# A linear-attention and ReLU network of four layers on one core: one more chunk of the first dense layer in seven block products, with the weight sums, the room of x and the GpSimd choices that go with it

## The chip, the cores and the metric

One NeuronCore of a Trainium2 chip runs the whole kernel. The metric is the device time of one execution in microseconds, as a median over runs. The core has a matrix engine (TensorE, PE in the profile, with PEld for its weight loads), a vector engine (VectorE, DVE), an activation engine (ScalarE, ACT), a general engine (GpSimd, POOL) and SyncE (SP), which here issues every DMA. The engines run their own instruction lists in order and wait for each other by semaphores.

## What is computed

The input x is 2048 x 512 in bf16. Four layers are applied: attention, dense, attention, dense, each on a layer norm of x and added to x. Both attention layers share their weights, and so do both dense layers. Cut to what matters:

```python
qkv = x @ wqkv                        # 32 heads of 16
phi = lambda t: where(t > 0, t + 1, exp(t)) + 1e-6
pq, pk = phi(q), phi(k)
kv  = einsum("bhsd,bhse->bhde", pk, v)
den = einsum("bhqd,bhd->bhq", pq, sum_s(pk))
A   = (einsum("bhqd,bhde->bhqe", pq, kv) / den) @ wo
B   = relu(x @ w1) @ w2               # 512 -> 1376 -> 512
x = x + A(layernorm(x)); x = x + B(layernorm(x))   # twice
```

## The kernel before

The 2048 rows are 16 tiles of 128, four tiles to a chunk, so four chunks 0 to 3. Layers are numbered 0 to 3; 0 and 2 are attention, 1 and 3 dense. x stays in SBUF as `xres` (f32); the bf16 input of layer 0 is `xin`, its normalised form `xn`, and the transposed form that TensorE needs `Tb`. All large intermediate values lie in `big`, cut into units of 512 columns: in attention layers the k features (16 units), the q features (16) and the spread reciprocal denominators (16); in dense layers the hidden values h, unit 4c + t for feature block c of 11 and chunk t.

An attention layer projects k for each tile and q for each chunk, forms G = xn' phi(k) (`a_g`), from it K'V under a mask and the product with `wo` (`a_kv`, `a_m`), the denominators (`a_den`), spreads their reciprocals over partitions by four DMAs for each chunk (`a_spread`, L779), scales q by them (`a_pqs`, L786), multiplies (`a_fin_mm`) and adds to x with the row sums for the next norm (`resid`, L657). The step `bar` of `layer_steps` is where the four chunks meet.

A dense layer forms h for each chunk (`h_step`) and then its output (`o_step`, `b_out`). The output, 256 x 256 blocks of rows and columns in a 2 x 2 scheme, is done in Winograd's form of Strassen's method: seven block products in place of eight, with sums of blocks made ahead of it by VectorE (`w2_sums` for the weights, `b_out_sums` for h) and after it from PSUM. For h there are two forms. `b_h` (L949) is the plain one: ten groups of four matmuls of 512 columns and a relu each. `b_h7` (L875) is the one in seven products: sums of the weights (`w1_sums`, L853), four sums of the transposed input (hs1 to hs4, L888), products of 256 columns, three of which are saved from PSUM by ACT (L926), VectorE adds (L913) and relus (L916, L917, L943, L945). Layer 3 uses it for all chunks and layer 1 from chunk `H7_FROM = 2` on. The last 96 of the 1376 features are apart (`b_h_rest`), turned by a DMA.

The sums of both weights lie in `xin`, in the room of x, which is free once layer 0's residual adds have read it; so they are made when layer 1 runs. One of the four sums of each weight overwrites a block of the weight itself: `usum3` puts b22 - b12 on b12 of w1.

What sets the order: the program writes out all operations with the buffers that they read and write, step by step in an order that `layer_steps` and the loop behind it set; `_list_schedule` (L218) then makes the instruction list of each engine. It is a list scheduler with a duration for every operation (the `C_` constants) and a delay to its consumer (`TAIL`). Among the next `WINDOW` operations of an engine by priority it takes the first that can start, else that with the earliest start. The priority is the operation's number plus an entry of the table `HINTS`; a key with `!` fixes which engine takes an operation that several can do (`add_flex`), by its place in the list of alternatives. Operations in `LOCKED` are laid out so that one on DVE and one on POOL do not overlap. SP's list, the DMAs, is made in the same way with a window of six. The first loads are written at L479 to L506, numbers 0 to 13: x tile 0, x tile 1, wk, x tiles 2 and 3, wq, x chunks 1, 2 and 3, wv, wvl, wo, w1, w2 in two parts.

Every matmul group is emitted at L653, every large GpSimd normalisation at L594; the table load of ACT is at L511.

Of the kernel before, what the change touches and what calls it, by code (L numbers as in the profile page):

```python
# [28 lines left out]
C_ACT_SB_AP = 710.0  # L29
# [17 lines left out]
TAIL = {PE: 150.0, ACT: 125.0, DVE: 80.0, POOL: 40.0, SP: 0.0}  # L47
# [4 lines left out]
WINDOW = {PE: 64, ACT: 80, DVE: 80, POOL: 12, SP: 6}  # L52


HINTS = {"0.bnag10": 2, "0.bnag14": 17, "0.bnst10": -271, "0.bnst12": 80, "0.bnst14": 51, "0.bnst15": 33, "0.bnst6": -82,
# [294 lines left out]
def build_kernel(nc, A_x, A_wqkv, A_wo, B_w1, B_w2, out, n_layers_pairs=2, K_STT=0, Q_STT=0, windows=None,  # L350
# [14 lines left out]
    EPS = 1e-5  # L365
    INV_D = 1.0 / D
    NLAYERS = 2 * n_layers_pairs
    UNITS = max(8 + 4, NFC) * NCH

    es = contextlib.ExitStack()  # L370
    with es:
# [1032 lines left out]
```

## Time and profile before

| | us |
|---|---|
| median of three runs | 268.98 |
| lowest, highest | 268.46, 270.23 |
| the profiled execution | 269.65 |
| its span in the profile | 267.9 |
| DMA: x tile 0 to w2's rest and x chunk 2 landed | 2.94 to 14.53 |

The span is what the profile shows from first to last instruction; some 1.7 us of the execution's time lie around it. The page gives for each engine the time in which at least one of its instructions ran. Rows with a mean in ns give the time of one instruction from start to end; instructions of an engine overlap their neighbours, so a start-to-start distance is shorter than such a row. A wait is put at the engine that stood still, with what released it behind the arrow.

### The profile page before, as it was taken

The numbers are of one execution on the slowest core, as the hardware profiler recorded it, in microseconds if no ns is written. First come the engines' busy times: TensorE is split into PE (matmuls) and PEld (weight loads), VectorE is DVE, ScalarE is ACT, GpSimd is POOL, SyncE is SP. The second block draws the span as 40 slices with busy tenths as digits, with TensorE's granted clock in tenths as the row PEclk, the third lists the DMA queues.
The fourth block names the chain that finished last, engine by engine and source line by source line (L and its number), as shares of the span: only waits on it lengthen the run. The fifth ranks groups of instructions, "written<-read, shape, count | busy, mean of one in ns | idle before, by whom it ended". The sixth has DMA issues, their size and how long they took to land.

```text
span 267.9 us, 5482 instructions
## 1 busy us (share of the span) xinstructions
PE 262.3 (98%) x2020; PEld 183.8 (69%) x2020; DVE 220.5 (82%) x612; ACT 192.0 (72%) x420; POOL 62.8 (23%) x158
## 2 busy tenths in 40 slices
PE   7999999999999999999999999999999999999995
PEld 3665446744646798768687745764488788898884
DVE  5799695679998799698889676348998989899994
ACT  4999987475994467689947599687899886475600
POOL 3210000015678014204005440000760830000000
PEclk9999999999999999999999999999999999999999
DMA  6904490644992400502202222063273221511012
GB/s 201 356 9 92 71 305 0 157 110 88 246 129 51 91 20 4 98 4 39 39 2 39 42 40 39 0 142 96 57 144 79 40 42 42 134 22 78 2 78 81
DMA packets 44890, 22.18 MB, mean 83 GB/s; under 512 B 34784, under 2 KB 43328, under 8 KB 44864
## 3 DMA queue, kind: packets, MB, share of 16 engines
q1 hardware_dynamic: 44864, 21.83, 34.5%
q8 instruction: 16, 0.26, 0.4%
q14 instruction: 10, 0.08, 0.1%
HBM read 7.14 MB, written 2.10 MB: 34 GB/s over the span
## 4 chain that ended last, share of the span: by engine, by line
PE 79%; ACT 8%; DMA 6%; DVE 5%; issue 0%; SPq 0%; DVEq 0%
PE ps L653 79%; DMA Tb<-xn 3%; ACT big L636 2%; ACT sqscr L668 2%; DMA wvl<-in_A_wqkv_dram 2%; DVE xres L660 2%; DMA xin<-in_A_x_dram 1%; ACT escr L638 1%; DVE big L789 1%; ACT Tb L624 1%; ACT xn L599 1%; DVE xn L590 1%; DVE bst L552 1%; ACT xres L638 1%; DVE xn L594 0%
## 5 line engine op out<-in xcount | busy, mean ns | idle before, releaser
L636 ACT ACTIVATE big<-ps 128x512 bf16<-128x512 f32 x64 | 39.7, 644 | 6.1 <-PE ps L653 5.8
L653 PE MATMUL ps<-Tb,w 128*128 128x256 f16 (+1 forms) x216 | 35.8, 304 | 0.1
L668 ACT ACTIVATE sqscr<-xres 128x512 bf16<-128x512 f32 x48 | 30.0, 626 | 6.9 <-DVE xres L1085 4.2
L653 PE MATMUL ps<-w,big 128*128 128x256 bf16 (+1 forms) x256 | 32.4, 272 | 0.0
L653 PE MATMUL ps<-wqkv,Tb 128*128 128x512 bf16 x128 | 31.2, 379 | 0.6 <-DMA Tb<-xn 0.6
L653 PE MATMUL ps<-big,xn 128*128 128x256 bf16 (+1 forms) x224 | 31.6, 288 | 0.0
L653 PE MATMUL ps<-Tb,wqkv 128*128 128x512 f16 (+1 forms) x144 | 31.4, 355 | 0.0
L638 ACT ACTIVATE escr<-ps 128x512 bf16<-128x512 f32 x48 | 29.9, 637 | 1.1 <-PE ps L653 1.1
L653 PE MATMUL ps<-Mf,big 128*128 128x512 bf16 x128 | 29.5, 379 | 0.0
L926 ACT ACTIVATE escr<-ps 128x512 f32<-128x512 f32 (+1 forms) x40 | 20.3, 540 | 11.2 <-PE ps L653 10.9
L653 PEld LDWEIGHTS ps<-w,big 128*128 128x128 bf16 (+1 forms) x256 | 25.0, 98 | 3.7
L653 PEld LDWEIGHTS ps<-big,xn 128*128 128x128 f16 x224 | 21.4, 98 | 8.8 <-issue 0.7
L653 PEld LDWEIGHTS ps<-Tb,w 128*128 128x128 bf16 x216 | 20.8, 98 | 9.5 <-DMA Tb<-xn 1.0
L913 DVE TENSOR_TENSOR big<-ps,escr 128x512 bf16<-128x512 f32 (+1 forms) x40 | 24.0, 606 | 3.7 <-PE ps L653 1.8
L599 ACT ACTIVATE xn<-xres,nbias,rstd 128x512 f16<-128x512 f32 x19 | 15.2, 810 | 9.6 <-POOL nbias L584 6.7
L653 PEld LDWEIGHTS ps<-Tb,wqkv 128*128 128x128 bf16 x144 | 13.9, 98 | 11.9 <-issue 0.2
L653 PEld LDWEIGHTS ps<-Mf,big 128*128 128x128 bf16 x128 | 12.2, 98 | 14.0 <-issue 0.7
L916 ACT ACTIVATE big<-big 128x512 bf16<-128x512 bf16 (+1 forms) x34 | 19.0, 569 | 3.2 <-DVE big L913 2.9
L646 DVE TENSOR_TENSOR big<-big,escr 128x512 bf16<-128x512 bf16 x48 | 19.8, 420 | 1.6 <-ACT big L636 1.1
L653 PEld LDWEIGHTS ps<-wqkv,Tb 128*128 128x128 f16 x128 | 12.1, 98 | 12.8 <-ACT escr L638 1.1
L1066 DVE TENSOR_TENSOR xres<-ps,xres 128x512 f32<-128x512 f32 x24 | 16.4, 685 | 4.6 <-PE ps L653 4.5
L640 DVE TENSOR_SCALAR escr<-escr 128x512 bf16<-128x512 bf16 x48 | 13.7, 287 | 7.7 <-ACT escr L638 7.2
(116 smaller groups left out, 525.2 us busy)
## 6 DMA issues: line engine op xcount, KB each, us to landing
big<-rdc SPq DMA_DIRECT2D x32, 128.0 KB, 2.6
wqkv<-in_A_wqkv_dram SPq DMA_DIRECT2D x3, 512.0 KB, 6.8
xin<-in_A_x_dram SPq DMA_DIRECT2D x3, 512.0 KB, 7.6
w<-in_B_w_dram SPq DMA_DIRECT2D x1, 1376.0 KB, 6.3
w<-in_B_w_dram SPq DMA_DIRECT2D x1, 1280.0 KB, 7.1
wo<-in_A_wo_dram SPq DMA_DIRECT2D x1, 512.0 KB, 7.2
out_dram<-GT SPq DMA_DIRECT2D x1, 512.0 KB, 2.6
out_dram<-Mf SPq DMA_DIRECT2D x1, 512.0 KB, 2.6
```

The lines of the kernel that those rows point to most:

```text
L599: (ACT, lambda e: e.activation(xn[:, i, :], src, ACTF.Identity, scale=rstd[:, i:i + 1], bias=nbias[:, i:i + 1]), C_ACT_SB_AP)],
L636: g.add(ACT, lambda e: e.activation(dst_ap, psv[:, b, :], ACTF.Identity, bias=1.0 + 1e-6, scale=1.0), [("ps", b)], [dst_key], C_ACT_PSUM, ...
L638: g.add(ACT, lambda e: e.activation(sap, psv[:, b, :], ACTF.Exp), [("ps", b)], skeys, C_ACT_EXP, name=name + "_exp")
L640: g.add(DVE, lambda e: e.tensor_scalar(sap, sap, 1.0, 1e-6, ALU.min, ALU.add), skeys, skeys, C_DVE_BF4X, name=name + "_em")
L646: g.add(DVE, lambda e: e.tensor_tensor(dst_ap, dst_ap, sap, ALU.max), [dst_key] + skeys, [dst_key], 340.0, name=name + "_phi")
L653: last = e.matmul(o, l, r, start=st, stop=sp, skip_group_check=skip)
L660: g.add(DVE, lambda e: e.scalar_tensor_tensor(xres[:, i, :], psv[:, b, :], 0.0, src, ALU.add, ALU.add, accum_out=s1[:, i:i + 1]), [("ps", ...
L668: g.add(ACT, lambda e: e.activation(sqscr[:, q, :], xres[:, i, :], ACTF.Square, scale=math.sqrt(INV_D), accum_out=s2[:, i:i + 1]), xr(i), ...
L913: g.add(DVE, lambda e: e.tensor_tensor(ap, sh(psv[:, bank, 0:w]), sh(other()), ALU.add), [("ps", bank)] + okeys + ([] if first else bk), q ...
L916: g.add_flex([(ACT, lambda e: e.activation(ap, ap, ACTF.Relu), C_ACT_PSUM if len(cs) == 2 else 270.0), (DVE, lambda e: e.tensor_scalar(ap, ...
L926: g.add(ACT, lambda e, w=w: e.activation(q[:, 0:w], psv[:, bank, 0:w], ACTF.Identity), [("ps", bank)], key, C_ACT_PSUM if len(cs) == 2 els ...
L1066: g.add(DVE, lambda e: e.tensor_tensor(dst, psv[:, bank, :].rearrange("p (a k) -> p a k", k=256), dst, ALU.add), [("ps", bank)] + keys, ke ...
```

## The change

It does the following, in the diff's order.

- `TAIL` of PE goes from 150 to 160, GpSimd's scheduling window from 12 to 40, and `HINTS` is replaced as a whole. A function gives the price that the scheduler puts on a two-input operation on GpSimd.
- Every ACT operation except the table load reads a key that the table load writes, so all come after it.
- `xin` is no tensor of its own; it is the last 16 of `big`'s 48 units. `tws` and `tw2s` hold the weight sums.
- h units of feature blocks 8 to 10 lie over x and carry its keys (`h_key`).
- The spread reciprocals go into `Tb`, in the tile places of their chunk, and no longer into `big`.
- Normalisations (of later layers), the scaling of q, the input sums, the weight sums and the sums of h may each go to DVE or GpSimd (the normalisations to ACT as well); until now every fourth normalisation was GpSimd's alone, and the others named were DVE's.
- `H7_FROM` is 1: chunk 1 of layer 1 is done in seven products.
- The weight sums are made in layer 0, in `bar` behind G of the last chunk, all but `usum3`, which is made right before chunk 1 of layer 1.
- The first step of h in layer 1 may be written out only after chunk 2 of layer 0 (after chunk 1 before). The output of chunk 0 need not come after all of layer 0 any more.

```diff
-TAIL = {PE: 150.0, ACT: 125.0, DVE: 80.0, POOL: 40.0, SP: 0.0}
+TAIL = {PE: 160.0, ACT: 125.0, DVE: 80.0, POOL: 40.0, SP: 0.0}
-WINDOW = {PE: 64, ACT: 80, DVE: 80, POOL: 12, SP: 6}
+def pool_tt(cols):
+    return 2.2 * cols + 90.0
+WINDOW = {PE: 64, ACT: 80, DVE: 80, POOL: 40, SP: 6}
...
+         "0.kv0_3": 145, "0.ld_w1": 204, "0.ld_wk": -3959, "0.ld_wvl": 180, "0.ld_x0": -25466, "0.ld_x1": -10725, "0.ld_x12":
+         34, "0.ld_x2": -6596, "0.ld_x4": -897, "0.m0": 64, "0.mev2": -340, "0.mev2!": 1, "0.nbias0!": 1, "0.nbias10": -300,
...
+         "3.hrrelu3!": 0, "3.hs1_0": -189, "3.hs1_2!": 1, "3.hs1_3": 271, "3.hs2_0": -42, "3.hs2_2!": 0, "3.hs2_3": 138,
+         "3.hs2_3!": 0, "3.hs3_1": 1616, "3.hs3_2": -117, "3.hs3_2!": 1, "3.hs3_3!": 0, "3.hs4_0": -151, "3.hs4_2!": 1,
+         "3.hs4_3!": 1, "3.hv5_0_0": 38, "3.hv5_1_2": 693, "3.m1_2": -578, "3.m1_3": 175, "3.m5_0": 307, "3.m5_1": 709,
...
+         "3.ssum3_1!": 0, "3.ssum3_2!": 1, "3.ssum3_3": -267, "3.ssum3_3!": 0, "3.ssum4_0!": 1, "3.ssum4_1!": 1, "3.ssum4_2!":
+         1, "3.ssum4_3!": 1, "3.ssum5_0": -56, "3.ssum5_1": -206, "3.ssum5_1!": 0, "3.ssum5_2": 166, "3.ssum5_2!": 0,
...
     def add(self, eng, emit, reads=(), writes=(), dur=100.0, lat=0.0, dma=False, name=""):
+        if eng == ACT and name != "table":
+            reads = list(reads) + [("lnw",)]
...
-    UNITS = max(8 + 4, NFC) * NCH
+    UNITS = 8 * NCH + NT
-        xin = sb("xin", [128, NT, 512], BF16)
-        H7_FROM = 2
+        H7_FROM = 1
+        xin = big[:, 8 * NCH * 512:UNITS * 512].rearrange("p (n d) -> p n d", d=512)
+        tws = sb("tws", [128, 3 * 1280], BF16)
+        tw2s = sb("tw2s", [128, 4096], BF16)
+        def h_key(u):
+            return [("big", u)] + ([("xin", u - 8 * NCH)] if u >= 8 * NCH else [])
...
-            if i % 4 == 3:
-                g.add(POOL, ts[1], xr(i) + [("rstd", i), ("mean", i)], [("xn", i)], ts[2], name="norm%d" % i)
-                return
-            g.add_flex([(DVE, ts[1], 530.0),
-                        (ACT, lambda e: e.activation(xn[:, i, :], src, ACTF.Identity, scale=rstd[:, i:i + 1], bias=nbias[:, i:i + 1]), C_ACT_SB_AP)],
+            g.add_flex([(DVE, ts[1], 470.0),
+                        (ACT, lambda e: e.activation(xn[:, i, :], src, ACTF.Identity, scale=rstd[:, i:i + 1], bias=nbias[:, i:i + 1]), C_ACT_SB_AP), ts],
...
-        def rb_unit(t, j):
-            return 32 + 4 * j + t
+        def rb_ap(t, j):
+            return Tb[:, 4 * t + j, :, :].rearrange("p c k -> p (c k)").bitcast(BF16)
+                dma(lambda e, j=j: e.dma_start(rb_ap(t, j), rdc[32 * j:32 * j + 32, t, :].unsqueeze(1).broadcast_to([32, 4, 512])),
+                    [("rdc", t)], [("T", 4 * t + j)], 650.0, "spread%d_%d" % (t, j), issue=620.0, late=late)
+                g.add_flex([(DVE, f, 340.0), (POOL, f, pool_tt(512))], [("T", 4 * t + j), ("big", u)], [("big", u)], name="pqs%d_%d" % (t, j))
...
-        def w1_sums():
+        def w1_sums(part):
+                if (nm == "usum3") == (part == 0) and part < 2:
+                    continue
+                g.add_flex([(DVE, f, C_DVE_SUM), (POOL, f, pool_tt(1280))], rd, wr, name=nm)
+                g.add_flex([(DVE, f, 340.0), (POOL, f, pool_tt(512))], rd, [wr], name="%s_%d" % (nm, t))
...
                 def bar():
                     g_a(NCH - 1)
+                    if first_layer:
+                        tw7.append(w1_sums(2 if H7_FROM == 0 else 0))
+                        w2_sums()
...
                 def o_step(t):
-                    if first_b and t == 0:
-                        w2_sums()
                     b_out(t, last_layer, sums[t])
...
                     if last_layer or t >= H7_FROM:
-                        if not tw7:
-                            tw7.append(w1_sums())
+                        if first_b and t == H7_FROM and t > 0:
+                            w1_sums(1)
                         b_h7(t, tw7[0])
...
-                    steps.append((1 if first_b and t == 0 else t, None, lambda t=t: h_step(t)))
+                    steps.append((2 if first_b and t == 0 else t, None, lambda t=t: h_step(t)))
-                        steps.append((NCH - 1 if first_b and t == 1 else None, None if last_layer else t - 1, lambda t=t: o_step(t - 1)))
+                        steps.append((None, None if last_layer else t - 1, lambda t=t: o_step(t - 1)))
```

More of the change, by code (lines that the diff above doesn't have):

```diff
@@ L367, in build_kernel @@
     NLAYERS = 2 * n_layers_pairs
-    UNITS = max(8 + 4, NFC) * NCH
+    UNITS = 8 * NCH + NT
+    assert NFC * NCH <= UNITS
     es = contextlib.ExitStack()
@@ L781, in a_spread @@
             for j in range(4):
-                u = rb_unit(t, j)
-                dma(lambda e, j=j, u=u: e.dma_start(unit_ap(u), rdc[32 * j:32 * j + 32, t, :].unsqueeze(1).broadcast_to([32, 4, 512])),
-                    [("rdc", t)], [("big", u)], 650.0, "spread%d_%d" % (t, j), issue=620.0, late=late)
+                dma(lambda e, j=j: e.dma_start(rb_ap(t, j), rdc[32 * j:32 * j + 32, t, :].unsqueeze(1).broadcast_to([32, 4, 512])),
+                    [("rdc", t)], [("T", 4 * t + j)], 650.0, "spread%d_%d" % (t, j), issue=620.0, late=late)
         def a_pqs(t):
             for j in range(4):
-                u, r = pq_unit(j, t), rb_unit(t, j)
-                g.add(DVE, lambda e, u=u, r=r: e.tensor_tensor(unit_ap(u), unit_ap(u), unit_ap(r), ALU.mult),
-                      [("big", r), ("big", u)], [("big", u)], 340.0, name="pqs%d_%d" % (t, j))
+                u = pq_unit(j, t)
+                f = (lambda e, u=u, j=j: e.tensor_tensor(unit_ap(u), unit_ap(u), rb_ap(t, j), ALU.mult))
+                g.add_flex([(DVE, f, 340.0), (POOL, f, pool_tt(512))], [("T", 4 * t + j), ("big", u)], [("big", u)], name="pqs%d_%d" % (t, j))
         def a_fin_mm(i, b, js):
@@ L858, in w1_sums @@
             b12, b22 = w1[:, 0:2, n:2 * n], w1[:, 2:4, n:2 * n]
-            def wk(lo, hi):
-                return [("xin", i) for i in range(lo, hi)]
             t1, t2, t4 = blk(0), blk(1), blk(2)
-            for (o, a, b, rd, wr, nm) in ((t1, b12, b11, [("w1",)], [("uw", 1)] + wk(0, 3), "usum1"),
-                                          (t2, b22, t1, [("w1",), ("uw", 1)], [("uw", 2)] + wk(3, 5), "usum2"),
+            for (o, a, b, rd, wr, nm) in ((t1, b12, b11, [("w1",)], [("uw", 1)], "usum1"),
+                                          (t2, b22, t1, [("w1",), ("uw", 1)], [("uw", 2)], "usum2"),
                                           (b12, b22, b12, [("uw", 1)], [("uw", 3), ("w1",)], "usum3"),
-                                          (t4, b21, t2, [("w1",), ("uw", 2)], [("uw", 4)] + wk(5, 8), "usum4")):
-                g.add(DVE, lambda e, o=o, a=a, b=b: e.tensor_tensor(o, a, b, ALU.subtract), rd, wr, C_DVE_SUM, name=nm)
+                                          (t4, b21, t2, [("w1",), ("uw", 2)], [("uw", 4)], "usum4")):
+                if (nm == "usum3") == (part == 0) and part < 2:
+                    continue
+                f = (lambda e, o=o, a=a, b=b: e.tensor_tensor(o, a, b, ALU.subtract))
+                g.add_flex([(DVE, f, C_DVE_SUM), (POOL, f, pool_tt(1280))], rd, wr, name=nm)
             return t1, t2, b12, t4
@@ L887, in b_h7 @@
                                               (s4_, a12, s2_, ALU.subtract, kl + [ks[1]], ks[3], "hs4")):
-                g.add(DVE, lambda e, o=o, a=a, b=b, op=op: e.tensor_tensor(o, a, b, op), rd, [wr], 340.0, name="%s_%d" % (nm, t))
+                f = (lambda e, o=o, a=a, b=b, op=op: e.tensor_tensor(o, a, b, op))
+                g.add_flex([(DVE, f, 340.0), (POOL, f, pool_tt(512))], rd, [wr], name="%s_%d" % (nm, t))
             def prod(name, bank, W, X, cs, opens, reads):
@@ L904, in quarter @@
                 us = [h_unit(c0 + p, t) for p in range(len(cs))]
-                return ap, [("bq", u, half) for u in us], [("big", u) for u in us]
+                return ap, [("bq", u, half) for u in us], [k for u in us for k in h_key(u)]
             def add(name, cs, bank, other, okeys, second, half, first):
@@ L966, in b_h @@
                              C_DVE_FLEX)],
-                           [("ps", b)], [("big", u)], name="hrelu%d_%d" % (t, c))
+                           [("ps", b)], h_key(u), name="hrelu%d_%d" % (t, c))
         xnb = xn[:].bitcast(BF16)
         HN = KH * 256
-        assert NFC == 2 * KH + 1 and FLAST < 128 and 3 * HN + 256 <= 4096 and HN <= 2048
+        assert KH == 5 and NFC == 2 * KH + 1 and FLAST < 128 and 3 * HN + 256 <= 4096 and HN <= 2048
         def xblk(o, n=KH):
-            return xinf[:, o:o + n * 256].rearrange("p (c k) -> p c k", k=256)
-        tw1, tw2, tw4 = xblk(4096), xblk(4096 + HN), xblk(4096 + 2 * HN)
-        tw1r = xinf[0:FLAST, 4096 + 3 * HN:4096 + 3 * HN + 256]
+            return tw2s[:, o:o + n * 256].rearrange("p (c k) -> p c k", k=256)
+        tw1, tw2, tw4 = xblk(0), xblk(HN), xblk(2 * HN)
+        tw1r = tw2s[0:FLAST, 3 * HN:3 * HN + 256]
         st_rdc = (rdc, lambda il, hf: [("rdc", il)])
@@ L982, in tt @@
         def tt(out_, a, b, op, reads, writes, dur, name):
-            g.add(DVE, lambda e: e.tensor_tensor(out_, a, b, op), reads, writes, dur, name=name)
+            cols = {C_DVE_SUM: 1280, 450.0: 768, 340.0: 512, 200.0: 256}[dur]
+            f = (lambda e: e.tensor_tensor(out_, a, b, op))
+            g.add_flex([(DVE, f, dur), (POOL, f, pool_tt(cols))], reads, writes, name=name)
         def w2_sums():
@@ L987, in w2_sums @@
             b12, b22 = w2[:, 0:KH, 256:512], w2[:, KH:2 * KH, 256:512]
-            xk = [("xin", i) for i in range(8, NT)]
-            tt(tw1, b12, b11, ALU.subtract, [("w2a",)], [("tw", 1)] + xk, C_DVE_SUM, "wsum1")
+            tt(tw1, b12, b11, ALU.subtract, [("w2a",)], [("tw", 1)], C_DVE_SUM, "wsum1")
             tt(tw2, b22, tw1, ALU.subtract, [("w2a",), ("tw", 1)], [("tw", 2)], C_DVE_SUM, "wsum2")
```

7 lines of the change are left out of this document (3 added, 4 removed), and 138 rows, old and new, of the table HINTS.

## The prediction

> **What bounds the kernel now.** I read the busy table of the page first, then the waits of TensorE, then stretches of the timeline.
>
> ```profile
> PE 262.3 (98%) x2020; PEld 183.8 (69%) x2020; DVE 220.5 (82%) x612; ACT 192.0 (72%) x420; POOL 62.8 (23%) x158
> ```
>
> TensorE is busy for all but 5.6 us of a 267.9 us span. A busy matmul can hide a stall, so its waits have to be read too:
>
> ```profile
> PE ps L521 <- DVE wrm L514: 1.2, 1, 1.2
> PE ps L618 <- DVE xn L590: 0.7, 2, 0.4
> PE ps L653 <- DMA Tb<-xn: 0.6, 1, 0.6
> ```
>
> Only the third lies behind the first 6.4 us. The stages, as a table of windows (columns: length, then the busy time of PE, PEld, DVE, ACT, POOL):
>
> ```profile
> 33.44:77.87 44.43, 44.28 (x292) 25.21 (x293) 36.44 (x112) 32.80 (x74) 12.83 (x31) 1.00 0.64 150
> 77.87:171.00 93.13, 93.13 (x713) 66.96 (x714) 75.58 (x225) 67.01 (x146) 26.00 (x65) 1.00 0.20 39
> ...
> 190.00:264.90 74.90, 74.89 (x692) 63.18 (x689) 69.24 (x153) 48.32 (x107) 16.14 (x35) 1.00 0.28 66
> ```
>
> The reader is to see three things: TensorE never pauses from 77.87 to 264.9, so time is won there only by giving it less to do; the granted clock is 1.00 throughout; VectorE has only 5.7 us left in the last stretch (74.90 - 69.24), so it is the next bound. The two pauses before that, in the timeline:
>
> ```profile
> 24.66 0.58 SPq L497 DMA_DIRECT2D wvl<-in_A_wqkv_dram  x1
> 30.12 2.62 SPq L604 DMA_TRANSPOSE Tb<-xn  x2
> 32.78 0.58 SPq L502 DMA_DIRECT2D w<-in_B_w_dram  x1
> ...
> 67.45 0.58 SPq L503 DMA_DIRECT2D w<-in_B_w_dram  x1
> 71.56 3.38 SPq L604 DMA_TRANSPOSE Tb<-xn  x2
> ```
>
> ```profile
> 29.34 0.43 DVE L679 TENSOR_TENSOR wqkv<-wqkv,wvl 128x512 bf16<-128x512 bf16 x1 [2.20 <-DMA wvl<-in_A_wqkv_dram]
> 33.44 2.75 PE L653 MATMUL ps<-wqkv,Tb 128*128 128x512 bf16 x12 [0.59 <-DMA Tb<-xn]
> ```
>
> First pause: VectorE stands 2.2 us for wvl (issued 24.66, landed 29.32), the chunk 3 normalisation behind it is late, its transpose starts at 30.12 and lands at 33.30, and TensorE waits 0.59 us. Second: w2, issued at 67.45, lands at 74.55; the chunk 1 transpose issued at 71.56 lands at 76.99, 5.4 us against 3.1 for most, and its pair, issued at 73.72, at 77.82. In the window from 77.3 to 77.9 TensorE is busy 0.45 of 0.60. A row shows a 512-column matmul as 0.379 us but the next starts 0.216 after it, so 0.16 us of each pause hides under the last busy bar: the pauses are 0.75 and 0.31 us.
>
> **The change, part by part.**
>
> *Fewer columns on TensorE.* Chunk 1 of the first dense layer has ten groups of four 512-column matmuls. The run at 77.87 takes 1.90 us for eight; (1.90 - 0.38) / 7 is 0.217, and the group starts, 77.87, 78.74, 79.61, are 0.87 apart: 40 x 0.216 = 8.64 us. In seven products they are 7 x 5 x 2 = 70 matmuls of 256 columns. In the last layer 15 of these take 1.80 us: (1.80 - 0.27) / 14 = 0.109, so 70 x 0.109 = 7.64 us. **-1.00 us**, on the path, since TensorE does not pause there. The smaller weight loads (98 ns each) still fit under 109 ns, as in the chunks that run this way now.
>
> *What the seven products need of the others.* From the rows of the six chunks that work so, per chunk: 9 saves (L926, 27.8 us in all / 6 = 4.6 on ACT), 9 adds from PSUM (L913, 32.1 / 6 = 5.4 on DVE), 9 relus (L916 and L917, 24.3 / 6 = 4.1, mostly ACT), 3 relus from PSUM (1.6), 4 sums of the input (L888, 12.2 / 6 = 2.0). Gone are ten relus, 8 on ACT and 2 on DVE (5.8). Net some 5 us on ACT and 7 us on DVE. From 80 to 100 ACT is busy 10.9 of 20 us, DVE 17.1. ACT has room. For DVE the next item pays. Nothing on the path while both hold; if DVE's cover is gone, it runs short by up to 7 - 2.9 = 4 us in those 20, of which the chunk's consumer sees little: chunk 1's first output product starts at 102.76, ten us after its last hidden one.
>
> *Weight sums moved forward.* Seven sums of 1280 columns (0.82 us a row, 0.735 from start to start) and two small ones leave the stretch 72 to 96, in which VectorE is full (from 60 to 70 it is busy 10.00 of 10), and go, less the one that overwrites w1, in front of layer 0's last stage: 7 x 0.735 + 0.35 = 5.5 us into 40 to 60, where VectorE has 20 - 12.8 = 7.2 us idle. Behind them in its queue stand the mask of K'V and the scaling of the queries, for which TensorE waits. Cost between 0 (all in idle time) and 2.9 us (four sums in a row in front of one such link); I take 0, as three quarters of the gap suffice. The one sum left, on b12, must now wait for chunk 0's products rather than chunk 1's; 0.82 us, with six other product groups (over 3 us) in front of its reader, as now: 0.
>
> *The loads on SP's queue.* Priorities put w2 and wo ahead of x's chunk 3. Now 1.6 MB (x chunk 3, the v weights, w2's rest, x chunk 2) land from 9.98 to 14.53, 358 GB/s; 1.8 MB more in front means x chunk 3 at 14.5 + 5.0 = 19.5 us. Its first statistics run at 19.71 and its last at 24.82: 0, with 0.2 us of room, 1 us if it fails. w2 no longer stands in front of chunk 1's transpose at 71.56: it lands 3.1 us after its issue, at 74.7, its pair at 76.8, before TensorE asks at 77.56. **-0.31 us**; next late would be the h remainder's transpose, 78.26 for a reader at 83.92. w1, on the other hand, moves up to right behind wvl, by the order of priorities that the diff gives, and so in front of chunk 3's transposes. w1 took 4.4 us (34.65 to 39.06) behind the transposes; a transpose behind a large load landed 2.4 us after it (74.55 to 76.99). Behind wvl, whose parts land from 26.8 to 29.3, w1 lands at 31.2 to 33.7 and the transpose at 33.6 to 36.1: 0.3 to 2.8 us later than 33.30. Were it in front, VectorE no longer held by wvl, it could land 2.4 us earlier and the 0.75 pause would go. What TensorE does in its place: from 36.9 on, by the kernel's order laid beside the timeline, it runs groups that need nothing of chunk 3 (g0_3_2, g0_2_2, g1_2_1, g1_2_2, qproj2_3, some 3.0 us), enough for 2.8 if they stand in front. I take neither gain nor loss: the pause stays at 0.75. Both ends, -0.75 and +2.8, are kept.
> The Trainium skill (DMA: Bandwidth & Descriptors, Queues, rings and completion order) says that on each DMA engine descriptors are consumed in ring order. By that rule w1 in front delays the transposes, as the row at 71.56 shows for w2; it gives rival A.
>
> *h in the room of x.* The units of h over x wait for the last reader of x, the residual add of tiles 0 to 11. Those run by 65 us and the first such relu at 70, so 0; were a residual late, chunk 0's last relus would stand behind it, at 0.6 us each. The first h step may be ordered only behind chunk 2, but TensorE already runs all but one group of chunk 3 before it. The spread of 1/denominator goes to Tb, whose last readers, the projections of the chunk, precede the denominator already: 16 DMAs of 128 KB with 2.6 us to landing per layer as now, 0.
>
> *The table load.* ACT already begins with it (1.05 to 2.34 us) and its next real work starts at 3.91 after 1.37 us idle. One more wait, on something done: 0.
>
> *Work that may go to GpSimd.* The hints put 4 input sums, 4 sums of 768 columns and one of 1280 of the last layer there, and may put more. No row shows a two-input operation of this size on GpSimd; the nearest is its normalisation:
>
> ```profile
> L594 DVE TENSOR_SCALAR xn<-xres,mean,rstd x17: 530/540/834, 62.6 to 197.6; 128x512 f16<-128x512 f32 x17
> L594 POOL TENSOR_SCALAR xn<-xres,mean,rstd x12: 766/772/1441, 64.5 to 219.5; 128x512 f16<-128x512 f32 x12
> ```
>
> 0.772 / 512 is 1.5 ns a column; a second input may double it. The nine have 6400 columns: 9.7 to 19.3 us of GpSimd, for 4.7 us saved on DVE (4 x 0.417 + 4 x 0.548 + 0.82). If DVE can work beside it, this is a gain of room and, TensorE being full, nothing in time. If DVE stands still meanwhile, it loses 5.0 to 14.6 us where 5.7 are idle: 0 to +8.9 us. I take 0, for the 772 median against a 766 minimum says that 12 pieces mostly ran undisturbed beside a DVE 90% busy; the one at 76.18 took 1.44 beside a 0.82 sum on DVE, and the DVE normalisation at 77.07, behind it, 0.83 against 0.54.
> The Trainium skill (SBUF — State Buffer, Who interferes with whom) states that a VectorE instruction with two SBUF inputs and a GpSimd instruction that reads SBUF exclude each other for a whole instruction; the 1.44 agrees. By that rule the moved sums and the like sums left on DVE take turns, which gives rival B. For the price of a two-input operation the Trainium skill's GPSIMD Engine Reference (Side-by-side cycle accounting) has 4497 ns for 2048 columns, by which the nine would take an estimated 14 us, inside the bounds above.
>
> *The whole order.* A new hints table, one window and one constant reorder every queue. TensorE's pauses in the old order, from 6.4 us on, sum to about 1.1 us besides small ones of 0.1; for the new one I bound the rest by 0 and by the 2.8 above, and take the old pattern less the 0.31.
>
> **Sum.** The profiled execution took 269.65 us, span 267.9 and 1.7 around it; the median of the three runs is 268.98, 0.67 less. 267.9 - 1.00 - 0.31 = 266.6 of span, 268.3 for an execution like that one, **267.7** against the median.
>
> **Rivals.**
> A. w1 in front of chunk 3's transposes with TensorE's order not filled: 267.7 + 2.8 = 270.5, slower than before. It decides from a landing of the transpose 1.3 us behind what TensorE has left to do. For: the priorities and the row at 71.56. Against: 3.0 us of other groups.
> B. VectorE becomes the bound of the last layer, taking turns with GpSimd. At the middle, 14.5 us lost, 14.5 - 4.7 - 5.7 = 4.1: 271.8. It decides where DVE loses over 5.7 us net. For: 9.96 busy of 10 from 220 to 230. Against: adds from PSUM are much of DVE's work there, and have one SBUF input.
> C. Better: the 0.75 pause goes as well, 267.0 (266.2 if the start gains too). For: w2 and wvl no longer stand in DVE's way. Against: w1.
> D. The change saves columns, but the pauses of the new order eat them: 269.0. For: DVE 82% busy, with little slack anywhere. Against: rows of 93 us without a pause.
>
> **How the numbers follow.** Forecast 0.40 (267.1 to 268.5 by itself), C 0.17, D 0.12, A 0.15, B 0.16. The range leaves out the low tail of C and the upper half of B, about 2 in 10 with what lies outside all cases: 266.5 to 271.8. One per cent, about what a measurement of this kernel can tell from no change, is 2.7 us. Faster than 266.3 needs both pauses gone and more: 0.07, from C. Slower than 271.7: half of B and A with B together, 0.15. Within: 0.78.
>
> **What would show it.** Right: 30 more matmul rows, 70 of 256 columns in place of 40 of 512; no wait on Tb near 77; PE busy in layer 1 down by 1.0; the table load first. For C or A: the landing of chunk 3's first transposes against 33.3 and a TensorE wait there. For B: DVE at 10 of 10 in all windows from 190, two-input rows on DVE over 0.42 and 0.82, TensorE waits on L983 or L888. The prediction is wrong if TensorE shows a pause of over 1 us anywhere behind 6.4 us, or if the seven-product matmuls do not keep their 0.109.

## The result, and the profile after

| | median us | lowest, highest | runs |
|---|---|---|---|
| before, beside it | 269.61 | 268.46, 270.80 | 6 |
| after | 273.35 | 272.83, 273.95 | 6 |

The change makes the kernel slower: the ratio of after to before is 1.0154, with a 95% interval of 1.0126 to 1.0183. The forecast was 267.7 and its range ended at 271.8. The profiled execution of after took 273.63 us, its span 271.9, which is 4.0 us more than before. Ratios here and below are made with runs of the kernel before on the same chip, round by round, and need not equal the quotient of two medians. One execution of the run e10 below took 305.88 us at a granted clock of 0.853; its median is that of the other nine, and its profile, which is of that execution, is not read.

The busy table of the page after:

```profile
PE 263.9 (97%) x2050; PEld 184.6 (68%) x2050; DVE 230.7 (85%) x626; ACT 185.7 (68%) x411; POOL 97.5 (36%) x177
```

The 30 more matmuls are there, ACT is busy 6.3 us less and VectorE 10.2 more, although 26 of its sums and scalings went to GpSimd, which has 34.7 us more. The waits of TensorE after (columns: us in total, times, longest):

```profile
PE ps L661 <- DVE big L921: 3.0, 5, 1.1
PE ps L532 <- DVE wrm L525: 1.2, 1, 1.2
PE ps L626 <- DVE xn L601: 0.3, 1, 0.3
PE ps L661 <- ACT lnd L934: 0.2, 1, 0.2
```

The wait for a transpose (`Tb<-xn`) is gone. In its place TensorE waits five times for an add of VectorE from PSUM, L921, which was L913. The stages after, as a table of windows (length, then the busy time of PE, PEld, DVE, ACT, POOL):

```profile
33.44:78.00 44.56, 44.56 (x294) 24.93 (x293) 39.45 (x115) 35.02 (x77) 22.41 (x35) 1.00 0.46 90
78.00:171.00 93.00, 91.86 (x733) 67.44 (x732) 77.82 (x228) 60.21 (x133) 35.03 (x68) 1.00 0.20 34
171.00:268.90 97.90, 95.60 (x830) 74.07 (x828) 84.17 (x191) 62.93 (x140) 34.48 (x55) 1.00 0.29 67
210.00:230.00 20.00, 18.08 (x159) 14.04 (x158) 19.83 (x40) 7.21 (x17) 7.69 (x6) 1.00 0.24 52
```

The first stretch has no idle TensorE any more. The second and third do, where there was next to none before, and from 210 to 230 VectorE is busy 19.83 of 20 us while TensorE has 1.9 us idle.

Since a busy bar hides part of a pause, I also took the start-to-start distances of all matmuls from 6.4 us on. At their undisturbed spacing (0.216, 0.109 and 0.056 us for 512, 256 and 128 columns) they sum to 259.83 us before and 258.66 after: -1.17. Of this, 1.01 is the 40 matmuls of 512 columns that became 70 of 256; the other 0.17 is three matmuls of 128 columns that start ahead of 6.4 us after and behind it before. Pauses of over 0.112 us beyond that spacing sum to 1.19 before and 5.56 after: +4.37. Smaller irregularities are +0.76. Together that is +3.96, the whole difference of the spans. By place, the 5.56 are 0 ahead of 55 us, 2.49 from 55 to 170, and 3.07 behind it. The longest are 1.24 and 1.00, behind the matmuls that start at 215.57 and 220.55; below, pauses are named by such starts.

What comes ahead of these pauses can be read on VectorE. One place, from the timeline after (start, length, engine; in brackets the idle time ahead of the row and what ended it):

```profile
214.23 1.75 POOL L992 TENSOR_TENSOR xn<-big,xn 128x768 bf16<-128x768 bf16 x1 [2.23 <-DVE xn L992]
214.41 1.85 DVE L992 TENSOR_TENSOR Tb<-big,xn 128x512 bf16<-128x512 bf16 x1
...
215.94 2.44 POOL L895 TENSOR_TENSOR xn<-Tb 128x512 f16<-128x512 f16 x2
216.19 0.68 DVE L921 TENSOR_TENSOR big<-ps,lnd 128x512 bf16<-128x512 f32 x1
...
216.92 0.61 PE L661 MATMUL ps<-Tb,tws 128*128 128x256 f16 x4 [1.08 <-DVE big L921]
...
217.39 1.15 DVE L925 TENSOR_SCALAR big<-big 128x512 bf16<-128x512 bf16 x1
```

A sum of 512 columns on VectorE starts 0.18 us behind a sum on GpSimd and takes 1.85 us, not 0.42. It ends 0.28 us behind GpSimd's end. The add that TensorE waits for stands behind it in VectorE's list. Such rows by their line after (min, median, max in ns):

```profile
L992 DVE TENSOR_TENSOR Tb<-big,xn x7: 409/415/1855, 84.1 to 263.6; 128x512 bf16<-128x512 bf16 x7
...
L992 DVE TENSOR_TENSOR xn<-big,xn x4: 544/548/1510, 84.4 to 152.1; 128x768 bf16<-128x768 bf16 x4
...
L992 POOL TENSOR_TENSOR xn<-big,xn x4: 1636/1694/1966, 214.2 to 261.8; 128x768 bf16<-128x768 bf16 x4
L992 POOL TENSOR_TENSOR big<-big x2: 2606/2614/2622, 148.8 to 247.9; 128x1280 bf16<-128x1280 bf16 x2
```

```profile
L983 DVE TENSOR_TENSOR Tb<-big,xn x8: 413/415/421, 84.7 to 257.3; 128x512 bf16<-128x512 bf16 x8
...
L983 DVE TENSOR_TENSOR xn<-big,xn x8: 544/548/554, 91.0 to 256.8; 128x768 bf16<-128x768 bf16 x8
```

The first fence is after, the second the same line before. The medians of the VectorE rows are equal; it is single rows that grow, where these two of before have none over 0.56. Taken over all rows of VectorE that exceed their group's median by over 0.08 us, the excess is 7.6 us after and 2.0 before. Eleven rows carry the 7.6 (six relus 3.0, five two-input sums 4.6), and each lies beside an operation of GpSimd that reads SBUF: ten beside two-input sums, one beside a normalisation. Nearly every cluster of pauses follows such a row in time: 79.39 (1.77 us, not 0.82) ahead of the pauses from 82.17; 88.88 and 89.55 (relus, 0.75 and 1.24, not 0.29) ahead of 90.88; 133.95 (1.51, not 0.55) ahead of 135.58; 204.17 (1.37, not 0.42) ahead of 205.58; 214.41 and 217.39 ahead of 215.57 and 220.55.

### The profile page after: what moved, and what is told of

The parts are those of the page before. It is cut to its first block, busy times and chain, and to the rows that moved or that the text cites. A ratio compares the mean times of both kernels' runs of the same rounds, so it can differ in the third digit from the quotient of the medians.

```text
span 271.9 us, 5596 instructions
## 1 busy us (share of the span) xinstructions
PE 263.9 (97%) x2050; PEld 184.6 (68%) x2050; DVE 230.7 (85%) x626; ACT 185.7 (68%) x411; POOL 97.5 (36%) x177
## 4 chain that ended last, share of the span: by engine, by line
PE 73%; DVE 14%; ACT 7%; DMA 3%; POOL 1%; issue 1%; SPq 0%; DVEq 0%; POOLq 0%
PE ps L661 72%; DVE big L921 5%; ACT escr L646 2%; ACT big L644 2%; DVE Tb L992 2%; DVE big L925 2%; ACT escr L934 1%; DMA Tb<-xn 1%; DVE xn L895 1%; DMA big<-in_A_x_dram 1%; DVE xn L992 1%; DVE xres L1075 1%; POOL var L589 1%; ACT sqscr L676 1%; PE ps L626 1%
## 5 line engine op out<-in xcount | busy, mean ns | idle before, releaser
L644 ACT ACTIVATE big<-ps 128x512 bf16<-128x512 f32 x64 | 42.3, 677 | 10.2 <-PE ps L661 10.2
L646 ACT ACTIVATE escr<-ps 128x512 bf16<-128x512 f32 x48 | 31.0, 673 | 0.5 <-PE ps L661 0.3
L921 DVE TENSOR_TENSOR big<-ps,escr 128x512 bf16<-128x512 f32 (+1 forms) x47 | 27.5, 599 | 4.2 <-ACT escr L934 3.5
L934 ACT ACTIVATE escr<-ps 128x512 f32<-128x512 f32 (+1 forms) x47 | 23.7, 539 | 8.7 <-PE ps L661 8.2
L661 PE MATMUL ps<-Tb,w 128*128 128x256 f16 (+1 forms) x196 | 29.3, 286 | 0.1
L924 ACT ACTIVATE big<-big 128x512 bf16<-128x512 bf16 (+1 forms) x30 | 16.5, 559 | 11.2 <-DVE big L921 11.1
L661 PEld LDWEIGHTS ps<-Tb,w 128*128 128x128 bf16 x196 | 18.5, 98 | 5.9 <-DMA Tb<-xn 1.1
L661 PEld LDWEIGHTS ps<-Mf,big 128*128 128x128 bf16 x128 | 12.1, 98 | 14.9 <-DVE big L796 0.9
L593 POOL TENSOR_TENSOR rstd<-veps,nhalf 128x2 f32<-128x2 f32 x24 | 18.5, 771 | 10.1 <-DVE veps L591 9.3
L654 DVE TENSOR_TENSOR big<-big,escr 128x512 bf16<-128x512 bf16 x48 | 19.5, 420 | 1.8 <-ACT big L644 1.2
L661 PE MATMUL ps<-xn,tws 128*128 128x256 f16 x140 | 20.4, 273 | 0.3 <-DVE big L921 0.3
L661 PEld LDWEIGHTS ps<-wqkv,Tb 128*128 128x128 f16 x128 | 12.1, 98 | 12.6 <-ACT xres L646 0.6
L661 PE MATMUL ps<-xn,w 128*128 128x256 f16 x140 | 20.4, 273 | 0.2 <-ACT lnd L934 0.2
```

Of the source, the lines that this page charges most:

```text
L593: g.add(POOL, lambda e: e.tensor_tensor(rstd[:, sl], veps[:, sl], nhalf[:, 0:n], ALU.pow), [("veps", lo), ("nhalf",)], [("rstd", i) for i ...
L644: g.add(ACT, lambda e: e.activation(dst_ap, psv[:, b, :], ACTF.Identity, bias=1.0 + 1e-6, scale=1.0), [("ps", b)], [dst_key], C_ACT_PSUM, ...
L646: g.add(ACT, lambda e: e.activation(sap, psv[:, b, :], ACTF.Exp), [("ps", b)], skeys, C_ACT_EXP, name=name + "_exp")
L654: g.add(DVE, lambda e: e.tensor_tensor(dst_ap, dst_ap, sap, ALU.max), [dst_key] + skeys, [dst_key], 340.0, name=name + "_phi")
L661: last = e.matmul(o, l, r, start=st, stop=sp, skip_group_check=skip)
L921: g.add(DVE, lambda e: e.tensor_tensor(ap, sh(psv[:, bank, 0:w]), sh(other()), ALU.add), [("ps", bank)] + okeys + ([] if first else bk), q ...
```

## The experiments

Theory T1: time is lost because GpSimd's operations of two inputs and VectorE's work take turns at SBUF, and TensorE waits for what VectorE has queued behind. In form T1a the loss comes from GpSimd's reading; in T1b from its slow results, which come late. Rival T2: the extra sums of seven products overload VectorE, wherever GpSimd works. Rival T3: the new order as such is worse.

| run | median us | ratio to before, 95% |
|---|---|---|
| e1_dve_only | 271.62 | 1.0112 (1.0080 to 1.0144) |
| e2_memset | 267.94 | 0.9977 (0.9955 to 0.9999) |
| e3_before_h7 | 278.18 | 1.0368 (1.0319 to 1.0417) |
| e4_before_pool | 273.99 | 1.0196 (1.0148 to 1.0243) |
| e5_lock_relu | 272.32 | 1.0110 (1.0051 to 1.0168) |
| e6_long_memset | 267.66 | 0.9961 (0.9936 to 0.9986) |
| e7_h7_reordered | 273.12 | 1.0159 (1.0114 to 1.0205) |
| e8_after_dve_reordered | 269.34 | 1.0021 (1.0002 to 1.0041) |
| e9_before_reordered | 269.64 | 1.0020 (1.0000 to 1.0040) |
| e10_memset_last | 270.10 | 1.0027 (0.9996 to 1.0059) |
| e11_after_dve_margin | 273.82 | 1.0147 (1.0084 to 1.0211) |
| e12_memset_first | 270.71 | 1.0049 (1.0023 to 1.0074) |

The medians of the kernel before beside them were 268.43 to 269.06.

### The 26 operations back on VectorE, in the order after: e1

```diff
+        for o in list(order[POOL]):
+            if any(x in o.name for x in ("pqs", "hs", "ssum", "usum", "wsum")):
+                order[POOL].remove(o); order[DVE].append(o); o.eng = DVE
+        order[DVE].sort(key=lambda o: (o.t_start, o.idx))
```

> The changed kernel in its own order; only the 26 two-input operations that it gives to GpSimd (sums of h and of the input, three scalings of q, one small weight sum) are put back on VectorE, at the place of their planned start. Theory 1 (VectorE stands still while GpSimd runs a two-input operation: 7.6 us of lengthened VectorE rows, of which TensorE sees 4.4 us of new pauses): the lengthened rows go, though VectorE gets some 9.5 us of work; TensorE's pauses of over 0.112 us fall from 5.6 to 1 to 3 us, time 269 to 271. Theory 2 (the seven products of chunk 1 overload VectorE) and theory 3 (the new order itself is bad): 273 or more, since VectorE has more to do in the same order.

271.62 us, a little over T1's range. VectorE's excess falls from 7.6 to 0.5 us, so the long rows belong to GpSimd's two-input operations. Yet the pauses of TensorE fall only to some 4.4 us. In its waits the add from PSUM is still the first line, at half the time:

```profile
PE ps L661 <- DVE big L921: 1.4, 2, 0.7
```

VectorE now has the 26 operations itself, in a list made for it without them. This order has no room for them. T1 alone does not account for the pauses that e1 still has.

### GpSimd writes but does not read: e2 and e6

```diff
-    def add_flex(self, alts, reads=(), writes=(), name=""):
+    def add_flex(self, alts, reads=(), writes=(), name="", out=None):
+        if out is not None:
+            alts = [a if a[0] != POOL else (POOL, (lambda e: e.memset(out(), 0.0)), a[2]) for a in alts]
```

e2 leaves out the 26 sums and scalings: GpSimd writes zeros to their places, at the same place in its list and with the same waits on both sides.

> The changed kernel, same instruction order, but each two-input operation on GpSimd is replaced by a memset of its result: it leaves out those sums and scalings, so its output is another one. GpSimd then reads no SBUF in them. Theory 1: VectorE's two-input rows are no longer lengthened; pauses of TensorE fall by 3 us or more, time 268.5 to 270.5. Theories 2 and 3: the pauses stay, 272.5 to 273.5.

267.94 us, 0.6 below T1's range and far from that of T2 and T3. From the busy table and the waits of e2:

```profile
PE 259.5 (98%) x2036; PEld 185.0 (70%) x2050; DVE 224.5 (85%) x626; ACT 185.7 (70%) x411; POOL 69.7 (26%) x177
```

```profile
PE ps L534 <- DVE wrm L527: 1.3, 1, 1.3
PE ps L628 <- DVE xn L603: 0.7, 2, 0.4
```

No wait on VectorE's adds is left. VectorE has the same 626 instructions as after and is 6.2 us shorter; one pause of 0.13 us remains. (The traces of e1, e2, e5, e6 and e12 hold 2036 of the 2050 matmul records, and each missing one leaves a gap of one matmul's length, 0.22 us, which is not counted as a pause.) But a memset of 0.52 us is also faster than the sum that it replaces (1.15 us for 512 columns), so e2 does not tell T1a from T1b. e6 keeps GpSimd busy longer with further memsets into spare columns, and the consumer waits for the last of them. Each of these operations also waits for the one ahead of it on GpSimd. GpSimd is busy 85.4 us, against 97.5 after and 69.7 in e2; of the 12.1 that lack, 8.3 are one small weight sum that took 8.63 us after and 0.31 here, and nobody waited for it. The other 25 take 31.3 us together, against 33.8:

```diff
+            def _long(e, d=...):                 # d: the price of the sum in the scheduler
+                for _ in range(min(4, max(0, int(round((d - 540.0) / 500.0))))):
+                    self.nsp = (self.nsp + 1) % 4
+                    e.memset(self.spare[:, 512 * self.nsp:512 * self.nsp + 512], 0.0)
+                return e.memset(out(), 0.0)
```

> As the memset run, the changed kernel's order with the two-input operations on GpSimd replaced by writes (those sums and scalings are left out), but GpSimd now writes long enough to be as long at work as before: one to four extra memsets of a scratch buffer, some 1.0 us for a sum of 512 columns. Theory 1a (what hurts is that GpSimd reads SBUF beside VectorE): time stays near the memset run's, 267.5 to 269.5, and VectorE's two-input rows keep their length. Theory 1b (what hurts is that GpSimd is slow and its result late): pauses come back, 271 or more.

267.66 us, and no pause of over 0.112 us from 6.4 us on. VectorE's rows beside these memsets keep their length:

```profile
L1001 DVE TENSOR_TENSOR Tb<-big,xn x7: 415/415/419, 82.4 to 257.3; 128x512 bf16<-128x512 bf16 x7
L1001 DVE TENSOR_TENSOR big<-big x6: 814/816/819, 81.6 to 253.6; 128x1280 bf16<-128x1280 bf16 x6
L1001 DVE TENSOR_TENSOR xn<-big,xn x4: 548/548/551, 82.7 to 149.0; 128x768 bf16<-128x768 bf16 x4
```

The maximum of 1855 ns is 419 here. T1a holds and T1b falls: what costs the time is that these operations read, not that their results are late. Both runs leave work out, so they bound what this order could reach, and are no kernels to use.

### One half of the places at a time: e10 and e12

The same edit as in e2, with `and self.layer == 3` (e10: only those of the last layer are left out) or `and self.layer < 3` (e12: only those of the first three). By the traces these are 12 and 14 operations; the expectations below say sixteen and ten, and chunks 0 to 2 where the list has two sums of chunk 3 as well.

> The kernel after in its own order, with GpSimd's sums of the last layer alone made into memsets (these sums of chunks 0 to 2 are left out); the ten operations of two inputs in the first three layers stay on GpSimd as they were. T1 says that the cost goes by the place where the two engines meet: the pauses behind 170 us (3.07 us in the kernel after) go, those between 55 and 170 us (2.49 us) stay, and the time is 270 to 271 us. If the time lost were not tied to the places (an order that is late throughout, T3), pauses would show up behind 170 us all the same, and the time would stay over 272 us.

> The counterpart of the run before: the kernel after in its own order, with GpSimd's ten sums and scalings of two inputs in the first three layers made into memsets (these are left out), the sixteen of the last layer on GpSimd as they were. T1: the pauses between 55 and 170 us (2.49 us) go, those behind 170 us (3.07 us) stay within 1 us, and the time is 270.3 to 271.5 us. T3: pauses stay in both parts, or the time stays over 272 us.

270.10 and 270.71 us, both times as T1 has them; whether e10's pauses go where T1 says is not shown by a trace. In e12 the pauses between 55 and 170 us are gone (2.49 to 0) and those behind 170 stay (3.07 to 3.31), as do the row that makes the longest of them, and the wait:

```profile
L994 DVE TENSOR_TENSOR Tb<-big,xn x7: 414/416/1853, 82.8 to 260.9; 128x512 bf16<-128x512 bf16 x7
```

```profile
PE ps L663 <- DVE big L923: 2.3, 3, 1.1
```

By the medians, against 273.35 after, the last layer's operations are worth 3.25 us, those of the first three 2.64, and all of them 5.41 (e2); by the ratios to before, 3.4, 2.8 and 4.8. The halves add up to the whole within 1.4 us, and lie near the pauses that after has in each (3.07 and 2.49). The loss is tied to the places where the two engines meet.

### The same operations moved in the kernel before: e4

```diff
+ON_POOL = ('1.hs3_2', '1.hs4_2', ..., '3.ssum3_2', '3.ssumr_2')   # 21 of the dense layers
+        for o in list(order[DVE]):
+            if o.key in ON_POOL:
+                order[DVE].remove(o); order[POOL].append(o); o.eng = POOL
+        order[POOL].sort(key=lambda o: (o.t_start, o.idx))
```

> The kernel before in its own order; 21 two-input operations that the changed kernel gives to GpSimd in the dense layers are given to GpSimd here too, nothing else. Theory 1: VectorE rows beside them are lengthened by some 5 us and TensorE pauses grow by 2 us or more: 271.5 to 274. Theories 2 and 3: VectorE has 7 us less to do and TensorE is fed as before, 269 to 270.

273.99 us: with chunk 1 in its plain form, the order and the loads of before, and none of the rest of the change, the move alone costs as much as the whole change. VectorE's excess is 12.1 us, against 2.0 before, which is twice the growth that theory 1 named:

```profile
L985 DVE TENSOR_TENSOR Tb<-big,xn x7: 411/418/2714, 84.6 to 261.0; 128x512 bf16<-128x512 bf16 x7
L985 DVE TENSOR_TENSOR big<-big x6: 812/942/1291, 81.0 to 262.5; 128x1280 bf16<-128x1280 bf16 x6
```

Some of it is also TensorE waiting for GpSimd itself (`POOL xn`, 1.0 us once), in an order not made for that.

### The relus kept apart by the scheduler: e5

```diff
-LOCKED = ("norm", "_em", "_phi", "pqs", "hs", "ssum", "usum", "wsum", "wvless", "madd")
+LOCKED = ("norm", "_em", "_phi", "pqs", "hs", "ssum", "usum", "wsum", "wvless", "madd", "hc11r", "hc12r", "hc22r")
```

> The changed kernel with the relus of the seven products added to the operations that its scheduler keeps apart from GpSimd's; the order is planned anew. Theory 1: the lengthened relu rows (4.1 of the 7.6 us) go or shrink, TensorE's pauses fall by 0.5 to 2 us, 271 to 273; those of two-input rows stay, as the scheduler knew of them and they happened all the same. Theory 1b or 3: no gain, 273 or more.

272.32 us, a small gain and in theory 1's range, but with an interval that overlaps that of after. The profiled execution, at 273.44 us the longest of the four, has pauses of some 5.5 us, so the fall of 0.5 to 2 is not seen there. (The relus are 3.0 of the 7.6 us, not the 4.1 of the expectation.) The relus' excess falls from 3.0 to 1.1 us and the longest relu from 1239 to 950 ns, but the two-input rows, which `LOCKED` has always held apart, still meet: the excess is 6.3 us. The scheduler lays them apart in its own time; the instruction lists carry the order of each engine only, and nothing in them makes one wait for the other.

### Seven products without GpSimd's reading: e3, e7, e8, e11, with e9 as control

e3 and e7 are the kernel before with one line changed (`H7_FROM = 1`), e3 with the old priorities, e7 with priorities searched anew. e8 and e11 are the kernel after with the GpSimd alternative of the 26 operations struck out, the relus in `LOCKED` as in e5, and priorities searched anew, e11 with 0.7 us more for each transpose. e9 is the kernel before with priorities searched anew. The search also fixes which engine takes an operation that several can do (`CHOICE`). What it found enters so, ahead of the scheduling (cut):

```diff
-        H7_FROM = 2                                   # e3, e7
+        H7_FROM = 1
+        if any(x in name for x in ("pqs", "hs", "ssum", "usum", "wsum")):   # e8, e11, in add_flex
+            alts = alts[:1]
+        for o in g.ops:                               # e7, e8, e9, e11
+            o.prio = PRIO[o.idx]
+            if o.idx in CHOICE:
+                o.eng, o.emit, o.dur = o.alts[CHOICE[o.idx]]
```

> The kernel before with one number changed: the seven products from chunk 1 of layer 1 on, weight sums still in the room of x and made there, planned by its own scheduler with its old hints. Theory 1: TensorE saves its 1.0 us and pauses grow by 0 to 1.5 for an order that was not made for it: 268.5 to 270. Theory 2: pauses between 78 and 105 us of 2 us or more, 271 to 273.

> The kernel before with chunk 1's first layer in seven products and nothing else of the change: the weight sums stay in the room of x, and every sum and scaling of two inputs stays on VectorE; the order is made anew by a search, since e3's was not. Theory T1 (GpSimd's reading beside VectorE costs the time): 267.5 to 269.0 us, VectorE's lengthened rows within 2 us in all as before, TensorE's pauses 1 to 2 us. Rival T2 (the extra sums of seven products overload VectorE, wherever GpSimd works): 270 us or more, pauses of 3 us or more that end with VectorE's rows.

> The kernel after, with its 26 sums and scalings of two inputs on VectorE as in e1, but with an order made anew for that by a search. T1: 268.0 to 270.0 us, below e1's 271.6, with VectorE's lengthened rows under 2 us and TensorE's pauses under 3 us. Rival T2 or T3 (seven products, or what the new order does to VectorE, is the cost): 271 us or more with pauses as in e1, 4 us or more.

> A control: the kernel before with its own operations, in another order found by the same search. If the order as such is worth little, 268.5 to 270.0 us; if any new order costs as much as the change did (T3), 271 us or more.

> As e8, the kernel after with all its sums and scalings of two inputs on VectorE, in another order, searched with 0.7 us more allowed for each transpose, since e7's pauses ended with transposes. If the saved columns of seven products come through once neither GpSimd nor a transpose stands in the way, 267.5 to 269.0 us; if VectorE's larger load alone makes pauses (T2), 270 us or more.

Of the four kernels in seven products three missed T1's numbers. e3 (278.18) has pauses of over 9 us, with 2.4 at 60.82 in layer 0, ahead of anything that seven products touch: its old priorities belong to another program, and it tells nothing of T2. e7 (273.12) has three pauses of 1.1, 1.9 and 1.3 us, and two of them end with a transpose in the waits, as does the idle time of VectorE ahead of the one of 1.9:

```profile
PE ps L581 <- DMA Tb<-xn: 2.0, 2, 1.1
PE ps L581 <- DVE big L841: 1.8, 1, 1.8
```

```profile
91.85 0.43 DVE L816 TENSOR_TENSOR xn<-Tb 128x512 f16<-128x512 f16 x1 [1.92 <-DMA Tb<-xn]
```

VectorE's excess is 1.4 us there; it stood idle for the transpose. Neither T1 nor T2 had named this. e11 (273.82) gave the transposes more time and paid with pauses of 6.0 us that end with six different releasers. e8 (269.34) is the one that came out as T1 has it:

```profile
78.00:171.00 93.00, 93.00 (x753) 70.08 (x752) 80.41 (x240) 64.88 (x140) 19.83 (x55) 1.00 0.21 38
171.00:264.20 93.20, 92.87 (x815) 72.67 (x813) 82.37 (x197) 57.42 (x128) 17.72 (x43) 1.00 0.30 70
```

It does all that after does, with 230.2 us of VectorE against 230.7, an excess of 0.6 us and pauses of 1.56 us. (The pauses of before sum to 1.19.) So VectorE can carry seven products and all sums and stop TensorE hardly more than before, and T2 falls as a limit. e8 shows that the work fits; order, choice of engines and `LOCKED` changed together there, so it does not tell which of them makes it fit. What remains of T2 is e1: in an order that has no room for them the 26 operations cost some three quarters as much on VectorE (4.4 us of pauses against 5.56). The control e9 shows that a new order need not cost anything; e7 and e11 are 4 to 5 us behind before without any two-input operation on GpSimd, so an order can cost as much. T3 is therefore no cause of after's loss (e2 and e6 run in just that order with no pause of over 0.13 us), but it is why moving the work back is no plain gain.

## Why the prediction was wrong, point by point

**The step that failed is "Work that may go to GpSimd": "I take 0."** The runs put about +5 us in its place (after against e2: 5.4 by the medians, 4.8 by the ratios), shown as 5.56 us of pauses against 0.13. That is against the same order with the 26 operations left out. Against e1 and e8, which do them all on VectorE, in the same order and in another, it is 1.7 and 4.0 by the medians, 1.1 and 3.6 by the ratios: in this order they were free on neither engine. The bounds kept for the term, 0 to +8.9, held it, but the range ended at 271.8, the middle of rival B, and the time came out in the half that was left out. The value was taken from the wrong row: GpSimd's normalisations have one input and a median of 772 against a minimum of 766, but that tells how long GpSimd takes beside VectorE, while the cost lies with VectorE beside GpSimd. The 834 ns row named in that step, beside a median of 540, was the row to go by. The rule of the Trainium skill (SBUF — State Buffer, Who interferes with whom) that a VectorE instruction with two SBUF inputs and a GpSimd instruction that reads SBUF exclude each other stood in the prediction with rival B, and the trace agrees: 415 to 1855 ns beside reading, 419 at most beside writing alone (e6).

The step also counted nine operations, all in the last layer, by the hints; 26 went, 12 of them in the last layer. Its estimate of 1.5 to 3 ns per column held: 1.69 us for 768 columns and 2.61 for 1280, the medians, are 2.2 and 2.0 ns.

**Rival B** had the mechanism, its side and nearly its size (271.8), and a chance of 0.16. Among its signs stood TensorE's waits on the sums themselves (L983, L888); they came one step later, on the add from PSUM that stands behind such a sum in VectorE's list (L921). Its place was too narrow: of the pauses, 3.07 us lie behind 170 and 2.49 in layers 0 and 1. Its condition, a net loss of VectorE of over 5.7 us in the last stretch, was wrong in kind. VectorE need not be full over 75 us; one row of 1.85 us in front of an add that TensorE needs is enough, as at 214.41.

**Fewer columns, -1.00.** Right: 30 more matmuls, and 1.01 us less at undisturbed spacing.

**w2 out of the way of chunk 1's transpose, -0.31.** Right: the wait near 77 is gone, and nothing else stands in SP's list there.

**The loads on SP, w1.** The order was read rightly. x's chunk 3 landed at 20.58, 1.1 us behind the 19.5 of the working, and no pause came of it. SP's timeline after:

```profile
22.70 0.58 SPq L508 DMA_DIRECT2D wvl<-in_A_wqkv_dram  x1
23.33 0.44 SPq L513 DMA_DIRECT2D w<-in_B_w_dram  x1
27.47 5.48 SPq L612 DMA_TRANSPOSE Tb<-xn  x2
```

w1, issued at 23.33, landed at 31.37. Chunk 3's first transpose, issued at 27.47, landed at 32.38, 4.9 us after its issue, where it took 3.2 before (30.12 to 33.30). So it stood behind w1, but as it was issued 2.7 us earlier it landed 0.9 us earlier; the second landed at 34.76, against 34.65 before. The delay of 0.3 to 2.8 us against 33.30 did not come, TensorE did not pause, and with that A did not come. The **first pause, kept at 0.75**, went away all the same, as rival C had it; with B's loss it could not be seen in the total.

**Seven products on VectorE and ACT, the weight sums, h over x, the table load: 0 each.** No pause lies ahead of 55 us, and e2 and e6 run with all of these and no pause of over 0.13 us. With the reading gone, the order after gives 267.7 to 267.9 (267.9 to 268.4 by the ratios, from 268.98), where the sum for C was 267.0 and the forecast 267.7; since e2 and e6 leave out work, this bounds these terms and does not measure each.

**"The whole order"** was taken as the old pattern of pauses. For the order by itself this was right (e2, e6); but that the scheduler's list holds a VectorE and a GpSimd operation apart was no reason to think that the chip does.

What stays open: whether any order in seven products beats the kernel before. e8, the best that does all the work, is at 1.0021 (1.0002 to 1.0041), and the saved microsecond did not show there.

## What to carry to other kernels

Before work is moved from VectorE to GpSimd, look at what VectorE does beside it: price the move by VectorE's longest rows next to GpSimd's, not by GpSimd's own, and by who stands behind such a row rather than by VectorE's mean load. A scheduler that keeps two engines apart in its own time does not keep them apart on the chip unless one waits for the other. A run in which GpSimd only writes, in the same places, for about as long, tells whether its reading is the cost.

## What the runs showed of the hardware

The relus on VectorE have one SBUF input (bf16 to bf16), and they were lengthened too: the longest before and after,

```profile
L917 DVE TENSOR_SCALAR big<-big x20: 216/283/313, 99.7 to 247.9; 128x512 bf16<-128x512 bf16 x12, 128x256 bf16<-128x256 bf16 x8
```

```profile
L925 DVE TENSOR_SCALAR big<-big x33: 214/280/1239, 86.5 to 256.0; 128x512 bf16<-128x512 bf16 x22, 128x256 bf16<-128x256 bf16 x11
```

while the adds with one input from PSUM and one from SBUF did not (680 and 684 ns in the median, 692 and 693 at most, after and before). Beside memsets the relus still reach 0.72 us (e6), the two-input sums do not grow. And the turns go both ways: GpSimd's first sum after, 256 columns that take 0.67 us elsewhere, took 8.6 us from 34.91, while VectorE ran one-input scalar operations and two-input sums and products without a gap; nobody waited for it.

```profile
L992 POOL TENSOR_TENSOR Tb<-big x4: 665/668/674, 131.4 to 250.4; 96x256 bf16<-96x256 bf16 x4
...
L992 POOL TENSOR_TENSOR tw2s<-w x1: 8632/8632/8632, 34.9 to 34.9; 96x256 bf16<-96x256 bf16 x1
```
